# Retention and gated MLP on one core: all weight blocks but three on the transfer queue of the groups, and fewer buffers for keys and decays

## The chip, the cores and the metric

One NeuronCore of one Trainium2 chip. The metric is the device time of one execution in microseconds (us), the median of several runs. "Span" is the time from the first to the last instruction of a profiled execution.

## What is computed

A retention layer (linear attention with a decay per head), then a gated MLP whose spatial weight mixes the positions of a sequence. Cut to what matters:

```python
# q, k, v: (4, 8, 768, 64)
for t in range(S):
    state = gamma * state + k[t] (outer) v[t]
    y[t] = scale * q[t] @ state
x = y as (4, 768, 512)
h = maximum(x @ w_in, 0)            # w_in (512, 1024)
u, v = h[..., :512], h[..., 512:]
v_n = (v - mean(v)) / sqrt(var(v) + 1e-6)
v_s = einsum('ts,bsd->btd', w_spatial, v_n) + b_spatial
out = (u * v_s) @ w_out             # w_out (512, 512)
```

## The kernel before, in words

The sequence of each of the 4 batches is cut into 6 chunks of 128 positions: 24 **groups**, G0 to G23. `load_group` (L197) loads one group with four transfers, all issued on SP: `qv` in two halves of 256 KB, `kk` (512 KB: the keys in two layouts) and `qd` (256 KB: decays). GpSimd (POOL) then scales the values in place, one instruction for each half (L214). `ret_set(g)` (S, L216) multiplies the scores of group g+1 and the state update of group g on TensorE (PE); VectorE (DVE) adds the state (L250) and masks the scores (L257). `ret_out(g)` (X, L259) multiplies the outputs; DVE scales them with `qd` (`xf`, L283), ScalarE (ACT) rounds them to `xh` (L286), POOL takes the residue `xl`. So qv of group g is free after X(g) on PE, kk after S(g) on PE, qd after `xf` of g on DVE.

The weights come as doubles. `load_double` (L, L134) loads one of 12 raw blocks of 512 KB (4 of w_inv, 4 of w_inu, 4 of w_out); `split_double` (C, L147) makes two 32-bit halves out of it: abs on ACT (`da`, L154), five instructions on DVE (L155 to L159), a cast on ACT (L160), a residue on DVE for the first four blocks and on POOL for the others, and the low half on POOL (L162). Blocks 0 to 5 have places of their own; the later ones share two staging buffers. `load_spatial` (K) loads the spatial weight (2.25 MB in six transfers `wst`), `split_spatial` (W) splits it with a cast on ACT (L187) and a residue on DVE (on POOL for the last one of 12).

The MLP: `mlp_v` (V, 12 matmuls of 512 columns) and `mlp_norm` (N) make the normalised v: relu on ACT (`vr`, L320), statistics on DVE (`bst`, `mv`), three tiny instructions on POOL (`rs`, `nb`), then the norm, `vnh` (L333) and `vnl` on ACT and DVE. `item` (I) does one unit: `mlp_u` (`u`, relu `ur` on ACT), `mlp_spatial` (`sp`, needs vnh and vnl of all six chunks and all of the spatial weight), `mlp_out` (`o`, needs a block of w_out). Three float32r matmuls stand for each product (high by high, high by low, low by high).

The words of `START`, `FIRST`, `REST` and `LAST` give the program order. A scheduler then orders each engine's instructions, but every load keeps its place among the loads of its queue (`keep_in_program_order`, L115 and L132), and so do the matmuls after START. A queue issues in order: a transfer whose buffer is not free holds back all that stand behind it on that queue. Groups go over SP's queue, weights over ACT's queue, in which the ACT instructions stand too. Stores of the output (L405) are issued on SP as well, and the scheduler places them.

Of the loads of a group, `QD_BUFS` and the `bufs` of `qv` and `kk` say how far ahead they may run; all three are 3 before.

Of the kernel before, what the change touches and what calls it, by code (L numbers as in the profile page):

```python
# [9 lines left out]
F32 = mybir.dt.float32  # L10
# [3 lines left out]
I64 = mybir.dt.int64  # L14
# [12 lines left out]


START = (
    "v m L0 G0 L1 L2 L3 G1 C0 C1 S-1 G2 L4 L5 C2 S0 X0 C3 S1 X1 G3 V0 C4 S2 X2 V1 C5 G4 K0 S3 X3 "  # L30
    "N0 V2 K2 N1 V3 G5 S4 X4 N2 K4 K5 V4 N3 B U5 X5 N4 V5 L6 L7 W00 W10 W20 N5 W30 W40 W50"
)
FIRST = (
    "C6 I0 G6 C7 L8 W01 C8 L9 I1 G7 W11 W21 Z5 C9 L10 I2 S6 W31 G8 C10 L11 I3 X6 S7 W41 W51 G9 C11 "
    "I4 X7 S8 G10 I5 X8 S9 G11 I6 X9 S10 G12 V0 V1 I7 X10 S11 N0 V2 N1 V3 N2 G13 X11 V4 N3 V5 N4 O7 "
    "N5"
)
# [4 lines left out]
LAST = "I0 I1 I2 I3 I4 I5 I6 I7 O7"  # L42


BLOCKS = [0, 1, 2, 3, 4, 5, 6, 8, 7, 9, 10, 11]
VECTOR_BLOCKS = 4
VECTOR_SPATIAL = 11
WARM_UP = 10
QD_BUFS = 3


@with_exitstack
def tile_retention_gmlp(
# [14 lines left out]
    nc = tc.nc  # L68
    P = 128
    B = out.shape[0]  # L70
    NG = kk.shape[0]
    NC = NG // B
    C = P // 2
    D = C
    NP = kk.shape[2] // (4 * D)
    S = NC * P
    KT = w_inv.shape[1]
    DM = KT * P
    NJ = KT
    HALF = S // 2  # L80
# [5 lines left out]
    rpool = ctx.enter_context(tc.tile_pool(name="ret", bufs=2))  # L86
    mpool = ctx.enter_context(tc.tile_pool(name="mlp", bufs=2))
# [6 lines left out]
    bsp_t = wpool.tile([P, S], F32, name="bsp_t")  # L94
# [7 lines left out]
    wsp_h = wpool.tile([P, NC, S], F32R, name="wsp_h")  # L102
    wsp_l = wpool.tile([P, NC, S], F32R, name="wsp_l")
# [10 lines left out]
    def load(dst, src):  # L114
        tc.keep_in_program_order(nc.sync.dma_start(dst, src))  # L115

    def residue(eng, out, whole, high):
        eng.tensor_tensor(out, whole, high.bitcast(F32), ALU.subtract)  # L118

    def pick(on_vector):  # L120
        return nc.vector if on_vector else nc.gpsimd

    doubles = [
        (w[:, k, 0], w[:, k, 1], src[:, k])
        for w, src in ((winv_w, w_inv), (winu_w, w_inu), (wout_w, w_out))
        for k in range(KT)
    ]
# [3 lines left out]
    def load_weight(dst, src):  # L131
        tc.keep_in_program_order(nc.scalar.dma_start(dst, src))  # L132

    def load_double(i):  # L134

        if i >= len(doubles):
            return
        if i < 6:
            tag = ("vnh", "vnl")[i // 3]
            if i % 3 == 0:  # L140
                raws[tag] = mpool.tile([P, 3, DM], I64, tag=tag, name=f"raw{i}", bufs=1)
            raws[i] = raws[tag][:, i % 3]
        else:
            raws[i] = mpool.tile([P, DM], I64, tag="raw", name=f"raw{i}")[:, :]
        load_weight(raws[i], doubles[i][2])

    def split_double(i):  # L147
        hi, lo, _ = doubles[i]
# [17 lines left out]
    def load_spatial(c):  # L166


        if c < 4:
            if c % 2 == 0:  # L170
                tag = ("xh", "xl")[c // 2]
                t = mpool.tile([P, 2, S], F32, tag=tag, name=f"wst{c}", bufs=3)
                load_weight(t, w_sp[:, c : c + 2])
                for i in range(2):
                    for half in range(2):
                        staged[c + i, half] = t[:, i, half * HALF : half * HALF + HALF]
        elif c < NC:
            for half in range(2):
                tag = ("t", "gh" if half else "gl")[c - 4]
                t = mpool.tile([P, HALF], F32, tag=tag, name=f"wst{c}_{half}")  # L180
                load_weight(t, w_sp[:, c, half * HALF : half * HALF + HALF])
                staged[c, half] = t[:, :]

    def split_spatial(c, half):
        cols = slice(half * HALF, half * HALF + HALF)
        whole = staged.pop((c, half))
        nc.scalar.copy(wsp_h[:, c, cols], whole)  # L187
        residue(pick(c + NC * half < VECTOR_SPATIAL), wsp_l[:, c, cols], whole, wsp_h[:, c, cols])

    queries = {}  # L190
    keys = {}
# [5 lines left out]
    def load_group(g):  # L197
        if g >= NG:
            return

        t = rpool.tile([P, 4, 2, NP, C], F32, tag="qv", name=f"qv{g}", bufs=3)
        kt = rpool.tile([P, 2, 2, NP, C], F32, tag="kk", name=f"kk{g}", bufs=3)
        qd = rpool.tile([P, NP, P], F32, tag="qd", name=f"qd{g}", bufs=QD_BUFS)
        for r in range(2):
            rows = t[ROWS[r], 2 * r : 2 * r + 2]
            load(rows.rearrange("p s i h c -> p (s i h c)"), qv[g, r])
        load(kt[:, :, :, :, :].rearrange("p s i h c -> p (s i h c)"), kk[g])
        load(qd, qdecay[g % NC])
        queries[g], keys[g], naturals[g] = (t[:, 2], t[:, 1]), kt[:, 0], kt[:, 1]
        values[g], decays[g] = (t[:, 0], t[:, 3]), qd  # L210
        for r in range(2):
            vd = vd_t[ROWS[r], g % NC].unsqueeze(3).broadcast_to([D, 2, NP, D])
            w = values[g][r][ROWS[r]]
            nc.gpsimd.tensor_tensor(w, w, vd, ALU.mult)  # L214
# [195 lines left out]
    def item(b, i):  # L410
# [21 lines left out]
        "O": lambda b, g, n: mlp_out(b, *units[n]),  # L432
        "m": lambda b, g, n: load(mask_t, mask),
        "v": lambda b, g, n: load(vd_t, vdecay),
        "B": lambda b, g, n: load_weight(bsp_t, b_sp),
    }

    def emit(text, b, g0):
# [85 lines left out]
```

## Time and profile before

| | |
|---|---|
| median of 3 runs | 439.87 us (438.54 to 441.08) |
| the profiled execution's own time | 439.42 us |
| its span | 437.6 us |
| PE busy | 383.7 us (88%) |
| DVE / POOL / ACT busy | 218.2 / 174.7 / 128.7 us |
| mean granted PE clock | 0.938 of full |
| moved by DMA | 47.44 MB |

In the page's 40 slices (10.9 us each) PE is at 8 tenths or less in most of the first twelve and at 9 or more nearly throughout after them, but for one slice around 240 us. DVE is at 9 from the third to the sixth slice. The rows further down are in us from the start of the span; "idle before" is the time that an engine stood before an instruction, and what ended it.

### The profile page before, as it was taken

Reading aid. Unit: us, or ns where it says so; the run is one execution under the profiler, and the core shown is the slowest. Engines: PE = TensorE matmul, PEld = TensorE weight load, DVE = VectorE, ACT = ScalarE, POOL = GpSimd, SP = SyncE. Lnnn points to the kernel's source line nnn. Section 1 sums busy time; section 2 is a strip of 40 time slices with the busy share of each in tenths; the row PEclk is TensorE's granted clock in tenths of the full one; section 3 lists DMA queues with packets and bytes.
Section 4 is the critical chain, followed back from the end, with each engine's and each line's share of the span. In section 5 each row is a group of like instructions: output and inputs, shape, how many; then the busy total and the mean of one; then the engine's idle time right before and its main releaser. Section 6 shows DMA issues by size and latency. Waiting matters only on the chain.

```text
span 437.6 us, 9093 instructions
## 1 busy us (share of the span) xinstructions
PE 383.7 (88%) x3786; PEld 338.0 (77%) x3786; DVE 218.2 (50%) x420; ACT 128.7 (29%) x231; POOL 174.7 (40%) x201
## 2 busy tenths in 40 slices
PE   3278964888897999999995799999999999999996
PEld 1156652787786988799994788898999988999995
DVE  4699995468775555455552223354554124322122
ACT  3122534433222114542112013451113124511212
POOL 1666765564544444634442222424352223211110
PEclk8588686889998999999999799999999999999999
DMA  8974659511244542164434500064441000100102
GB/s 245 284 246 122 195 191 272 173 48 54 94 121 124 158 154 61 63 193 121 146 99 148 166 0 1 0 191 124 124 121 73 0 1 0 73 0 1 73 0 73
DMA packets 17417, 47.44 MB, mean 108 GB/s; under 512 B 2528, under 2 KB 3296, under 8 KB 17376
## 3 DMA queue, kind: packets, MB, share of 16 engines
q1 hardware_dynamic: 14640, 37.81, 28.6%
q10 hardware_dynamic: 2736, 9.05, 6.7%
q8 instruction: 30, 0.49, 0.5%
q14 instruction: 11, 0.09, 0.1%
HBM read 40.56 MB, written 6.29 MB: 107 GB/s over the span
## 4 chain that ended last, share of the span: by engine, by line
PE 75%; DMA 9%; DVE 7%; POOL 3%; issue 2%; ACT 2%; SPq 1%; POOLq 0%; DVEq 0%; ACTq 0%
PE sp L110 21%; PE v L110 15%; PE o L110 14%; PE u L110 14%; PE s L110 6%; PE x L110 5%; DMA qv<-in_qv_dram 3%; DMA qd<-in_qdecay_dram 2%; DMA raw<-in_w_inu_dram 2%; DVE qv L257 1%; DMA kk<-in_kk_dram 1%; DVE df L157 1%; DMA raw<-in_w_out_dram 1%; POOL xl L118 1%; DVE qv L250 1%
## 5 line engine op out<-in xcount | busy, mean ns | idle before, releaser
L214 POOL TENSOR_TENSOR qv<-qv,vd_t 64x512 f32<-64x512 f32 x48 | 54.3, 1132 | 57.1 <-DMA qv<-in_qv_dram 49.8
L118 POOL TENSOR_TENSOR gl<-t,gh 128x384 fp32r<-128x384 f32 x31 | 31.5, 1016 | 111.5 <-ACT gh L380 110.4
L110 PE MATMUL u<-xh,winu_w 128*128 128x384 f32 x256 | 72.6, 347 | 1.9 <-POOL winu_w L162 1.9
L110 PE MATMUL sp<-wsp_h,vnh 128*128 128x384 f32 x192 | 64.9, 338 | 3.2 <-ACT ur L354 3.2
L110 PE MATMUL v<-winv_w,xh 128*128 128x512 f32 x192 | 65.4, 423 | 0.9 <-POOL winv_w L162 0.7
L110 PE MATMUL o<-wout_w,gh 128*128 128x512 f32 x192 | 61.1, 398 | 5.0 <-POOL wout_w L162 5.0
L110 PE MATMUL sp<-wsp_h,vnl 128*128 128x384 f32 x192 | 64.9, 338 | 0.0
L110 PE MATMUL sp<-wsp_l,vnh 128*128 128x384 f32 x192 | 64.9, 338 | 0.0
L378 DVE TENSOR_TENSOR t<-sp,bsp_t 128x384 f32<-128x384 f32 (+1 forms) x34 | 18.0, 534 | 90.9 <-PE sp L110 90.8
L110 PEld LDWEIGHTS u<-xh,winu_w 128*128 128x128 f32 x256 | 47.3, 190 | 3.9 <-POOL winu_w L162 2.3
L110 PE MATMUL s<-qv,kk 64*64 64x64 f32 x1440 | 31.5, 233 | 17.6 <-DMA kk<-in_kk_dram 13.2
L110 PEld LDWEIGHTS v<-winv_w,xh 128*128 128x128 f32 x192 | 38.8, 206 | 9.8 <-POOL winv_w L162 0.8
L110 PE MATMUL v<-winv_w,xl 128*128 128x512 f32 x96 | 40.7, 424 | 5.7 <-POOL xl L118 5.7
L110 PEld LDWEIGHTS o<-wout_w,gh 128*128 128x128 f32 x192 | 36.0, 189 | 11.6 <-POOL wout_w L162 5.8
L110 PEld LDWEIGHTS s<-qv,kk 64*64 64x64 f32 x1440 | 27.7, 144 | 21.5 <-issue 19.4
L380 ACT CAST gh<-t 128x384 fp32r<-128x384 f32 (+1 forms) x34 | 16.6, 493 | 92.5 <-DVE t L379 90.1
L257 DVE TENSOR_TENSOR qv<-s,mask_t 64x256 f32<-64x256 f32 x92 | 38.6, 420 | 10.1 <-PE s L110 8.7
L110 PE MATMUL u<-xl,winu_w 128*128 128x384 f32 x128 | 43.3, 338 | 0.0
L118 POOL TENSOR_TENSOR xl<-xf,xh 128x512 fp32r<-128x512 f32 x24 | 31.3, 1303 | 29.7 <-ACT xh L286 29.7
L110 PEld LDWEIGHTS x<-qv 128*64 128x64 f32 (+1 forms) x768 | 27.9, 146 | 16.5 <-DVE qv L250 8.3
L110 PEld LDWEIGHTS sp<-wsp_h,vnh 128*128 128x128 f32 x192 | 36.6, 191 | 3.6 <-ACT ur L354 3.5
L110 PE MATMUL x<-qv 128*64 128x64 f32 (+1 forms) x768 | 32.9, 236 | 6.4 <-DVE qv L250 6.1
(57 smaller groups left out, 525.9 us busy)
## 6 DMA issues: line engine op xcount, KB each, us to landing
qv<-in_qv_dram SPq DMA_DIRECT2D x48, 256.0 KB, 4.3
kk<-in_kk_dram SPq DMA_DIRECT2D x24, 512.0 KB, 5.6
qd<-in_qdecay_dram SPq DMA_DIRECT2D x24, 256.0 KB, 5.5
out_dram<-ot SPq DMA_DIRECT2D x23, 256.0 KB, 2.0
raw<-in_w_inv_dram ACTq DMA_DIRECT2D x4, 512.0 KB, 6.9
raw<-in_w_inu_dram ACTq DMA_DIRECT2D x4, 512.0 KB, 7.0
raw<-in_w_out_dram ACTq DMA_DIRECT2D x4, 512.0 KB, 3.8
wst<-in_w_sp_dram ACTq DMA_DIRECT2D x2, 768.0 KB, 6.2
```

Of the source, the lines that this page charges most:

```text
L110: ins = nc.tensor.matmul(out, lhs, rhs, start=start, stop=stop)
L118: eng.tensor_tensor(out, whole, high.bitcast(F32), ALU.subtract)
L157: nc.vector.scalar_tensor_tensor(fi, top, -0x40000000, ai, ALU.bitwise_and, ALU.bitwise_or)
L214: nc.gpsimd.tensor_tensor(w, w, vd, ALU.mult)
L250: nc.vector.tensor_tensor(dst, u, w[r][ROWS[1 - r], i], ALU.add)
L257: nc.vector.tensor_tensor(m[r][ROWS[r], i], ts[i][col, 0], mk, ALU.mult)
L378: nc.vector.tensor_tensor(t[:, c], pp[:, c], bsp_t[:, tc_], ALU.add)
L380: nc.scalar.copy(gh[:, c], t[:, c])
```

## The change

- Raw blocks 0 to 8, the spatial weight and `b_sp` are loaded on SP's queue, among the groups; raw blocks 9 to 11 stay on ACT's queue (`FIRST_QUEUE`).
- Raw blocks from 6 on have three staging buffers where they had two.
- `kk` and `qd` have two buffers where they had three.
- START and FIRST are written anew: groups 1 to 5 come later between the weights, group 6, the spatial weight, and raw blocks 6 to 8 are loaded within START, and 9 to 11 early in FIRST. REST and LAST stay.
- The last residue of the spatial weight goes from POOL to DVE.

```diff
 START = (
-    "v m L0 G0 L1 L2 L3 G1 C0 C1 S-1 G2 L4 L5 C2 S0 X0 C3 S1 X1 G3 V0 C4 S2 X2 V1 C5 G4 K0 S3 X3 "
-    "N0 V2 K2 N1 V3 G5 S4 X4 N2 K4 K5 V4 N3 B U5 X5 N4 V5 L6 L7 W00 W10 W20 N5 W30 W40 W50"
+    "v m L0 G0 C0 L1 L2 S-1 C1 G1 L3 C2 S0 X0 G2 C3 L4 L5 S1 X1 K0 V0 C4 G3 S2 X2 K2 V1 C5 N0 G4 L6 "
+    "S3 X3 V2 N1 G5 W00 W10 K4 K5 S4 X4 V3 N2 W20 W30 B V4 N3 L7 U5 X5 W40 W50 N4 V5 G6 N5 L8"
 )
 FIRST = (
-    "C6 I0 G6 C7 L8 W01 C8 L9 I1 G7 W11 W21 Z5 C9 L10 I2 S6 W31 G8 C10 L11 I3 X6 S7 W41 W51 G9 C11 "
+    "C6 L9 I0 C7 W01 L10 C8 I1 G7 W11 W21 Z5 L11 C9 I2 S6 W31 G8 C10 I3 X6 S7 W41 W51 G9 C11 "
...
+FIRST_QUEUE = 9
 VECTOR_BLOCKS = 4
-VECTOR_SPATIAL = 11
+RAW_BUFS = 3
+KK_BUFS = 2
 WARM_UP = 10
-QD_BUFS = 3
+QD_BUFS = 2
...
-            raws[i] = mpool.tile([P, DM], I64, tag="raw", name=f"raw{i}")[:, :]
-        load_weight(raws[i], doubles[i][2])
+            raws[i] = mpool.tile([P, DM], I64, tag="raw", name=f"raw{i}", bufs=RAW_BUFS)[:, :]
+        (load if i < FIRST_QUEUE else load_weight)(raws[i], doubles[i][2])
...
-                load_weight(t, w_sp[:, c : c + 2])
+                load(t, w_sp[:, c : c + 2])
...
-                load_weight(t, w_sp[:, c, half * HALF : half * HALF + HALF])
+                load(t, w_sp[:, c, half * HALF : half * HALF + HALF])
...
-        residue(pick(c + NC * half < VECTOR_SPATIAL), wsp_l[:, c, cols], whole, wsp_h[:, c, cols])
+        residue(nc.vector, wsp_l[:, c, cols], whole, wsp_h[:, c, cols])
...
-        kt = rpool.tile([P, 2, 2, NP, C], F32, tag="kk", name=f"kk{g}", bufs=3)
+        kt = rpool.tile([P, 2, 2, NP, C], F32, tag="kk", name=f"kk{g}", bufs=KK_BUFS)
...
-        "B": lambda b, g, n: load_weight(bsp_t, b_sp),
+        "B": lambda b, g, n: load(bsp_t, b_sp),
```

PE's order stays nearly the same. Three places show what moves elsewhere. Numbers behind names are the group or block (`qv3` is of G3) and a buffer's serial number; lines of the changed kernel are three higher than before.

**SP's queue from group 2 on.** Before, groups alone:

```order
L115 DMA qv2_166<-in_qv_dram 64x1024 x2
L115 DMA kk2_167<-in_kk_dram 128x1024
L115 DMA qd2_168<-in_qdecay_dram 128x512
L115 DMA qv3_327<-in_qv_dram 64x1024 x2
L115 DMA kk3_328<-in_kk_dram 128x1024
```

In the changed kernel:

```order
L118 DMA qv2_242<-in_qv_dram 64x1024 x2
L118 DMA kk2_243<-in_kk_dram 128x1024
L118 DMA qd2_244<-in_qdecay_dram 128x512
L118 DMA raw3_164<-in_w_inu_dram 128x512 x2
L118 DMA wst0_327<-in_w_sp_dram 128x1536
L118 DMA qv3_366<-in_qv_dram 64x1024 x2
L118 DMA kk3_367<-in_kk_dram 128x1024
L118 DMA qd3_368<-in_qdecay_dram 128x512
L118 DMA wst2_438<-in_w_sp_dram 128x1536
```

Two raw blocks (4 and 5, in one tile named raw3) and a third of the spatial weight now stand between groups 2 and 3, and qd2 ahead of them waits for `xf` of group 0.

**DVE around the output of group 1.** Before:

```order
L250 TENSOR_TENSOR qv2_166<-s1_1_265,qv1_113 64x256 x2
L257 TENSOR_TENSOR qv2_166<-s1_1_265,mask_t_73 64x256 x2
L283 TENSOR_TENSOR xf1_323<-x1_306,qd1_115 128x512
L155 TENSOR_SCALAR da4_362<-da4_362 128x512
L321 BN_STATS bst0_0_352<-vr0_0_351 128x6
```

In the changed kernel:

```order
L253 TENSOR_TENSOR qv2_242<-s1_1_265,qv1_155 64x256 x2
L260 TENSOR_TENSOR qv2_242<-s1_1_265,mask_t_73 64x256 x2
L121 TENSOR_TENSOR wsp_l_81<-wst0_327,wsp_h_80 128x384 x4
L286 TENSOR_TENSOR xf1_323<-x1_306,qd1_157 128x512
L158 TENSOR_SCALAR da4_355<-da4_355 128x512
```

Four residues of the spatial weight, which need the transfer wst0, now stand ahead of `xf` of group 1; four more follow around group 2 and four around group 4.

**ACT from the relu of the last two v chunks to the first units.** Before:

```order
L320 ACTIVATE vr0_5_763<-v0_5_750 128x512
L132 DMA raw6_774<-in_w_inu_dram 128x512
L332 ACTIVATE vr0_4_699<-vr0_4_699,nb0_4_708,rs0_4_702 128x512
L132 DMA raw7_776<-in_w_out_dram 128x512
L333 CAST vnh0_336<-vr0_4_699 128x512
L154 ACTIVATE da6_793<-raw6_774 128x512
L332 ACTIVATE vr0_5_763<-vr0_5_763,nb0_5_772,rs0_5_766 128x512
L333 CAST vnh0_336<-vr0_5_763 128x512
L154 ACTIVATE da7_869<-raw7_776 128x512
L354 ACTIVATE ur0_0_0_817<-u0_0_0_804 128x384
```

In the changed kernel:

```order
L135 DMA raw9_815<-in_w_out_dram 128x512
L323 ACTIVATE vr0_5_779<-v0_5_766 128x512
L157 ACTIVATE da8_888<-raw8_802 128x512
L357 ACTIVATE ur0_0_0_830<-u0_0_0_817 128x384
L335 ACTIVATE vr0_4_710<-vr0_4_710,nb0_4_719,rs0_4_713 128x512
L357 ACTIVATE ur0_1_0_845<-u0_1_0_832 128x384
L335 ACTIVATE vr0_5_779<-vr0_5_779,nb0_5_788,rs0_5_782 128x512
L336 CAST vnh0_329<-vr0_4_710 128x512
L163 CAST wout_w_82<-df7_874 128x512
L336 CAST vnh0_329<-vr0_5_779 128x512
```

Raw blocks 6 and 7 were issued here and used at once; now they, and block 8, are loaded before, and only blocks 9 to 11 are issued from here on.

## Rows read from the trace of the kernel before

**Rows 1.** Busy time by stretch: PE, PEld, DVE, ACT, POOL, PE clock, DMA, GB/s
```profile
5.75:10.00 4.25, 0.00 (x0) 0.00 (x0) 3.63 (x8) 1.72 (x3) 0.00 (x0) 0.79 1.05 294
10.00:20.00 10.00, 1.61 (x36) 1.26 (x36) 6.42 (x9) 1.06 (x3) 8.36 (x6) 0.50 1.03 287
20.00:26.72 6.72, 3.98 (x95) 3.73 (x97) 6.41 (x15) 1.79 (x4) 3.37 (x3) 0.60 0.94 286
26.72:35.49 8.77, 6.29 (x112) 4.58 (x111) 8.42 (x15) 2.34 (x4) 5.30 (x4) 1.00 0.49 145
35.49:70.28 34.79, 26.22 (x370) 19.74 (x370) 33.18 (x60) 13.38 (x25) 21.65 (x23) 0.80 0.65 193
```

**Rows 2.** What PE waited for from 60 to 140 us: total, times, longest
```profile
PE v L110 <- POOL xl L118: 5.1, 1, 5.1
PE o L110 <- POOL wout_w L162: 5.0, 2, 3.4
PE sp L110 <- ACT ur L354: 3.2, 1, 3.2
PE u L110 <- POOL winu_w L162: 1.9, 1, 1.9
```

**Rows 3.** Chain of waits over the first 160 us: start, duration, what
```profile
73.76 8.18 PE v L110 x22
...
81.97 4.26 DMA raw<-in_w_inu_dram
...
93.83 4.25 DMA raw<-in_w_inu_dram
...
100.52 3.81 DMA raw<-in_w_out_dram
```

**Rows 4.** Chain of waits from 215 to 246 us
```profile
216.44 1.09 PE s L110 x64
...
237.17 5.74 DMA kk<-in_kk_dram
```

**Rows 5.** Timeline of ACT: the first raw blocks, and chunk 5's norm
```profile
0.72 1.86 ACTq L132 DMA_DIRECT2D raw<-in_w_inv_dram  x4
...
86.82 0.80 ACT L332 ACTIVATE vr<-vr,nb,rs 128x512 f32<-128x512 f32 x1
87.66 0.62 ACT L333 CAST vnh<-vr 128x512 fp32r<-128x512 f32 x1
...
88.74 0.86 ACT L354 ACTIVATE ur<-u 128x384 f32<-128x384 f32 x2
```

**Rows 6.** Timelines of SP (first group, a steady turn) and DVE (that turn)
```profile
1.64 1.17 SPq L115 DMA_DIRECT2D qv<-in_qv_dram  x2
...
208.03 0.58 SPq L115 DMA_DIRECT2D kk<-in_kk_dram  x1
...
206.89 0.69 DVE L283 TENSOR_TENSOR xf<-x,qd 128x512 f32<-128x512 f32 x1 [2.00 <-PE x L110]
```

**Rows 7.** Issues of `kk` in 0 to 15 and 140 to 230 us: median us to landing
```profile
kk<-in_kk_dram SPq DMA_DIRECT2D x2, 512.0 KB, 8.6
...
kk<-in_kk_dram SPq DMA_DIRECT2D x8, 512.0 KB, 5.0
```

**Rows 8.** DVE's groups to 90 us, by shape: busy, mean ns, idle before
```profile
L118 DVE TENSOR_TENSOR wsp_l<-wst,wsp_h 128x384 fp32r<-128x384 f32 x11 | 7.0, 654 | 5.3 <-ACT wsp_h L187 5.2
```

**Rows 9.** Timeline of POOL: `xl` of chunk 4, and the scaling of group 9
```profile
72.45 1.26 POOL L118 TENSOR_TENSOR xl<-xf,xh 128x512 fp32r<-128x512 f32 x1
...
128.52 2.49 POOL L214 TENSOR_TENSOR qv<-qv,vd_t 64x512 f32<-64x512 f32 x2 [2.11 <-DMA qv<-in_qv_dram]
```

**Rows 10.** Timeline of PE: ends of the first `sp` and of the second `o`
```profile
94.10 0.34 PE L110 MATMUL u<-xh,winu_w 128*128 128x384 f32 x1
...
113.75 1.16 PE L110 MATMUL s<-qv,kk 64*64 64x64 f32 x64
```

**Rows 11.** Chain near the end: two `u` units
```profile
375.60 4.19 PE u L110 x24
```

## The prediction

> **What bounds the kernel now.** I first read the busy time by stretch, to split the program into stages, then what PE waited for, then the chain of waits, and last the timelines of POOL, ACT and SP at the places that the change touches. After some 140 us PE is the bound and the change adds nothing to its work, so all that can be won lies before. There are two stages in it.
>
> In the first, up to the end of `xf` of the sixth chunk at 70.28 us, VectorE is the bound. From its first weight instruction at 5.75 it is busy 3.63 + 6.42 + 6.41 + 8.42 + 33.18 = 58.06 of 64.53 us; from 20 us on it idles 2.3 us in all [rows 1]. DMA is not: it moved 286 GB/s until 26.7 us and then only 145 and 193 [rows 1].
>
> In the second, from 70 to 134 us, PE waits for things that come late: 5.1 us for `xl` behind POOL, 3.2 for a relu that ACT reaches late, 1.9 for a block of w_inu and 5.0 for two of w_out [rows 2]. The chain says why: the three raw blocks on it are each issued only when they are due, and their transfers take 4.26, 4.25 and 3.81 us with the split behind them [rows 3]. A further stop stands at 237 us, where group 18 waits behind stores on SP's queue [rows 4]; REST and the order of those stores are unchanged, so I leave it as it is.
>
> **The change part by part.**
>
> *Start of the program.* The first raw block was issued on ACT at 0.72 [rows 5]. It now comes third on SP, where the third issue stood at 1.64 [rows 6]: 0.9 us later. DVE so starts near 6.7. In exchange one raw block instead of four stands ahead of the first group. DVE's idle time before 20 us, 0.6 + 3.6 in [rows 1], mostly goes: up to the first `xf` it has 16.5 us of the same work, so I place that at 23.5 with 0.3 us for waits, where it was 26.7.
>
> *The first stage after it.* qd2 waits for this `xf`, since `qd` has two buffers, and behind it stand 1.0 MB of raw blocks and 0.75 MB of the spatial weight. A group's 1.0 MB takes 1.16 us of issue and 5.0 to land [rows 6, 7]; less 3.5 us for its bytes at 286 GB/s [rows 1] this leaves 2.7 us for start and landing. So the first third of the spatial weight is there at 23.5 + 2.7 + 2.0 MB at 286 GB/s (7.0) = 33.2, and its first cast by 33.7. DVE takes its next 8.8 us of work [rows 1], reaches the four residues moved ahead of the second `xf` at 32.3, and waits 1.4 us. They cost 4 x 0.654 = 2.6 [rows 8], so the second `xf` starts at 36.3 against 35.49. From there the same 34.8 us follow, again with eight residues in them: 71.1, where it was 70.28. **The 3 us won at the start are spent on four residues and a wait: the first stage gives about nothing.** Bounds: DVE without any gap would end at 6.7 + 58.06 + 2.6 = 67.4, 3 us better; the other end is a rival below. I stay near 71, because the wait is worked out from a measured rate. What is won is work done ahead: all spatial residues but none late, and raw blocks 6 to 8 loaded.
>
> *Chunk 4's `xl`.* Before it ended at 72.45 + 1.26 = 73.71 [rows 9], since POOL had to scale groups 6 and 7 first. Now only group 6 stands ahead. Its qv goes out behind qd5, the last third of the spatial weight, the bias and raw block 7: 2.4 MB after the fourth `xf`, which I place at 55.5. That is 55.5 + 2.7 + 8.4 = 66.6, and scaling takes 2.5 [rows 9]: 69.1. The fifth `xf` and its cast come near 68. With up to 1 us of slack `xl` ends at 71.4: **2.3 us earlier.** The 22 matmuls behind it took 8.18 [rows 3], which I keep.
>
> *From the last v to the end of the first `sp`.* This was 94.10 - 81.94 = 12.2 us [rows 3, 10]; ACT stood before the abs of raw block 6 until its transfer, issued there, had landed. Now nothing in ACT's order waits for a transfer there. Two u units take 4.2 at full clock [rows 11]; behind the second one ACT does a relu (0.43), a norm (0.80), two casts of v and one of a weight (3 x 0.62) [rows 5], DVE a residue (0.7), PE the last matmul: 8.4 us. **3.8 us earlier.** At least 4.2 + 3.1 are needed by PE alone, at most it stays as it was.
>
> *To the end of the second `o`.* 113.75 - 94.10 = 19.65 us [rows 10] with the waits for blocks of w_inu (1.9) and w_out (5.0 - 3.4 = 1.6) in them [rows 2]. Block 8 is there early; 9 to 11 are issued on ACT some 20 us ahead of their matmuls, into three buffers. Both waits go: **3.5 us earlier.** If the splits rather than the transfers set them, nothing goes.
>
> *The last wait, 3.4 us.* The low half of the last w_out block stands on POOL behind the scaling of group 9 (2.49 us, after 2.11 us idle for its transfer) [rows 9]. Now that qv goes out behind qd8, which waits for an `xf` (0.7) and moves 0.9 us of bytes; the block's residue, 1.3 us, moves ahead of the scaling. I take nothing for it; it can at most give back the 3.4.
>
> *Fewer buffers later.* In a steady turn kk was issued at 208.03. Now qd of the group before goes first, after an `xf` that ends at 207.58 [rows 6]; with 0.4 and 1.2 us of issue kk goes at 209.2 and lands by 214.2 to 215.1, with qd's bytes ahead. Its scores are due at 216.44 [rows 4]. Hidden, by 1.3 to 2.2 us; if this cover were gone, PE would wait in every turn. The buffer of kk itself is free 1.1 us after X, earlier than this. The residue of the spatial weight moved to DVE costs 0.65 in the first stage, within the 2.6 above.
>
> The sum: -2.3 - 3.8 - 3.5 = -9.6, against the profiled execution's 439.42 (span 437.6 plus 1.8 around it): **429.8 us**. That execution lies 0.45 under the median of 439.87, so the changed kernel's median may as well be 430.
>
> **The rivals.**
>
> *More goes.* DVE closes all gaps of the first stage (3.0) and the wait for the last w_out block goes too (3.4): 423.4. For it: POOL does that block's residue earlier. Against: qd2's place on the queue.
>
> *One queue delays the groups.* With ACT's and SP's queues both loaded, a kk took 8.6 us to land against 5.0 in a quiet stretch [rows 7], so bytes are shared in the start either way. In one queue group 3 stands behind all 1.75 MB of weights. Were it served in turn with them it would be through after 2.5 MB instead of 3.0: 1.75 us at 286 GB/s. If groups 3, 4 and 5 each come that much after DVE wants them, 5.2 us go: 435.0. Against: I have kk3 and kk4 there about when DVE comes to them. The Trainium skill states such a service in turn ("DMA: Bandwidth & Descriptors", section "Queues, rings and completion order"): each DMA engine alternates packet by packet between the queue rows that have work, so that two queues share and one queue does not. By that rule the old queues favoured the groups and this change takes that away; no run here shows one row alone in the start.
>
> *Slower: the short buffers.* If kk needs over 216.44 - 209.2 = 7.2 us to land in the steady turns, PE stops in each. With the crowded 8.6 [rows 7] that is 1.4 us in each of 11 such groups, 15.4 in all: 439.42 - 9.6 + 15.4 = 445. Against: 5.0 was measured there with the same bytes.
>
> *The early loads do not help.* The blocks are there, but ACT, in order, has block 8's abs ahead of the first relu, and that waits for a buffer which POOL frees behind the scaling of groups 7 and 8. If those land 6 us later than I think, the second stage's 7.3 us shrink to 1, and the first gives nothing: about 438.5.
>
> **How the numbers follow.** My forecast has 0.50 (425.5 to 433), more goes 0.15, one queue delays 0.17, early loads do not help 0.10, slower 0.08. A difference within 0.5%, 2.2 us, can hardly be told from no change. Faster by more: 0.50 + 0.15 + 0.17 = 0.82. Within: 0.09. Slower: 0.09, with the tail of the fourth case. The range takes in the forecast, most of "more goes" and the delayed queue: 422.5 to 437.
>
> **What would show it.** In the changed profile DVE should be busy from 7 to 70 us nearly without a gap but for 1 to 2 us before a residue of the spatial weight near 33. No raw block should stand on the chain after 75 us. PE's waits for `ur`, for winu_w and the shorter one for wout_w should be gone, and the second `o` should end near 104. The stop of group 18 should stand unchanged, some 10 us earlier. I am wrong if kk or qv appears among PE's waits in the steady turns, if `xf` of the sixth chunk ends after 74 or before 67, or if waits for winu_w and wout_w remain with no transfer behind them.

## The result and the profile after

The changed kernel takes **442.10 us** (median of 20 runs, 439.64 to 446.42) against 439.96 for the kernel before in the same session: a ratio of 1.0049, with an interval from 1.0026 to 1.0072. That is 0.5% slower, where 429.8 was forecast and 437 was the end of the range. The profiled execution took 439.64 us with a span of 437.8, 2.5 us under that median, so its stages show where time moved rather than the exact sum.

| | before | forecast | after |
|---|---|---|---|
| end of the first `xf` | 26.72 | 23.5 | 26.89 |
| end of the second `xf` | 36.18 | 37.0 | 42.64 |
| end of the sixth `xf` | 70.28 | 71.1 | 80.17 |
| from there to the end of the second `o` | 43.47 | 33.05 | 37.27 |
| end of the second `o` | 113.75 | 104.15 | 117.44 |

Between the sixth `xf` and the second `o` it gained 6.2 us where 10.4 were forecast; up to the sixth `xf` it lost 9.9, and an end of that `xf` after 74 was one of the prediction's own signs of being wrong. Of the 3.7 us that are late at the second `o`, this execution makes up 3.5 by its end (0.8 at the last w_out block, 1.0 at the stop of group 18, the rest spread over the turns); by the medians it is less. The windows of the first stage show how. Columns are PE, PEld, DVE, ACT, POOL, PE clock, DMA share, GB/s, as in [rows 1]. Before:

```profile
22.00:28.00 6.00, 4.37 (x141) 4.03 (x136) 5.68 (x13) 2.02 (x4) 3.85 (x4) 0.72 0.89 287
28.00:38.00 10.00, 7.41 (x118) 5.67 (x118) 9.72 (x16) 2.50 (x4) 5.91 (x5) 0.88 0.54 143
38.00:44.00 6.00, 4.69 (x44) 3.56 (x42) 5.82 (x12) 1.22 (x2) 4.60 (x6) 0.92 0.43 141
```

In the changed kernel:

```profile
22.00:28.00 6.00, 2.17 (x64) 2.04 (x64) 5.78 (x12) 1.28 (x2) 3.58 (x4) 0.50 0.06 22
28.00:38.00 10.00, 5.90 (x52) 4.17 (x46) 6.51 (x12) 0.79 (x2) 2.23 (x2) 0.84 1.01 299
38.00:44.00 6.00, 3.30 (x81) 3.14 (x82) 5.62 (x8) 3.25 (x7) 3.10 (x3) 0.54 0.10 29
```

Twice for 6 us the DMA engines move 22 and 29 GB/s, and in between 299, with VectorE (DVE) idle for a third of those 10 us, where it was busy 9.72 of them before. (Idle DMA engines need not cost anything: before, they moved 4 GB/s from 33 to 36 us, with DVE busy 2.85 of those 3 us.) SP's timeline in the changed kernel tells why:

```profile
19.64 0.33 SPq L118 DMA_DIRECT2D kk<-in_kk_dram  x1
26.91 0.33 SPq L118 DMA_DIRECT2D qd<-in_qdecay_dram  x1
27.30 0.90 SPq L118 DMA_DIRECT2D raw<-in_w_inu_dram  x2
28.24 0.43 SPq L118 DMA_DIRECT2D wst<-in_w_sp_dram  x1
28.84 1.19 SPq L118 DMA_DIRECT2D qv<-in_qv_dram  x2
30.13 0.69 SPq L118 DMA_DIRECT2D kk<-in_kk_dram  x1
42.66 0.33 SPq L118 DMA_DIRECT2D qd<-in_qdecay_dram  x1
```

kk2 goes out at 19.64, then nothing for 7 us: qd2 is next, and its buffer is that of qd0, which the first `xf` reads until 26.89. Behind it stand the raw blocks, the spatial weight and group 3. The same recurs with qd3 at 42.66, behind the second `xf`. DVE's timeline shows the price; the last bracket is idle time and what ended it:

```profile
38.38 3.66 DVE L121 TENSOR_TENSOR wsp_l<-wst,wsp_h 128x384 fp32r<-128x384 f32 x4 [3.65 <-ACT wsp_h L190]
41.96 0.68 DVE L286 TENSOR_TENSOR xf<-x,qd 128x512 f32<-128x512 f32 x1
```

The third of the spatial weight issued at 28.24 landed at 37.8; DVE stood 3.65 us before its first residue, with the second `xf` behind it, and four residues took 3.66 us where [rows 8] gave 2.6. How long PE waited for `kk` ahead of scores (`s`) up to 60 us, before and in the changed kernel (total, times, longest):

```profile
PE s L110 <- DMA kk<-in_kk_dram: 5.7, 2, 4.1
PE s L113 <- DMA kk<-in_kk_dram: 16.2, 3, 6.5
```

What it waited for from 60 to 140 us, where [rows 2] stood, in the changed kernel:

```profile
PE v L113 <- ACT xh L289: 4.3, 1, 4.3
PE sp L113 <- ACT vnh L336: 2.7, 1, 2.7
PE o L113 <- POOL wout_w L165: 2.6, 1, 2.6
PE s L113 <- DMA kk<-in_kk_dram: 2.0, 1, 2.0
PE sp L113 <- ACT ur L357: 1.6, 1, 1.6
```

The wait for winu_w is gone and that for wout_w fell from 5.0 to 2.6 us, where 3.4 was forecast; that for `ur` fell only from 3.2 to 1.6, and the wait for `vnh` is new. POOL's timeline shows what was late there:

```profile
87.76 1.18 POOL L217 TENSOR_TENSOR qv<-qv,vd_t 64x512 f32<-64x512 f32 x1 [0.46 <-DMA qv<-in_qv_dram]
88.91 1.26 POOL L165 TENSOR_TENSOR winu_w<-df,da 128x512 fp32r<-128x512 f32 x1
90.26 0.23 POOL L326 TENSOR_SCALAR rs<-mv 128x1 f32<-128x1 f32 x1
90.57 1.04 POOL L217 TENSOR_TENSOR qv<-qv,vd_t 64x512 f32<-64x512 f32 x1
...
94.67 0.27 POOL L329 TENSOR_SCALAR nb<-mv,rs 128x1 f32<-128x1 f32 x1
```

The last v's relu ended at 87.2, and its `nb` only at 94.9: on POOL the tiny statistics stand behind the scaling of group 8, whose transfer was issued at 80.64 behind a held qd7 (80.20), and behind a weight's sum.

### The profile page after: what moved, and what is told of

Same layout as the page of the kernel before. It is cut to its first block, busy times and chain, and to the rows that moved or that the text cites. A ratio compares the mean times of both kernels' runs of the same rounds, so it can differ in the third digit from the quotient of the medians.

```text
span 437.8 us, 9095 instructions
## 1 busy us (share of the span) xinstructions
PE 383.7 (88%) x3786; PEld 338.7 (77%) x3786; DVE 229.8 (52%) x421; ACT 128.9 (29%) x231; POOL 173.5 (40%) x200
## 4 chain that ended last, share of the span: by engine, by line
PE 66%; DVE 12%; DMA 9%; POOL 4%; issue 4%; ACT 3%; SPq 1%; POOLq 0%; DVEq 0%; ACTq 0%
PE sp L113 21%; PE u L113 15%; PE o L113 14%; PE v L113 8%; PE s L113 4%; PE x L113 4%; DMA qv<-in_qv_dram 4%; DMA wst<-in_w_sp_dram 3%; DVE qv L260 2%; DVE wsp_l L121 2%; POOL qv L217 1%; DVE xf L286 1%; DVE df L160 1%; DMA raw<-in_w_inv_dram 1%; SPq L118 1%
## 5 line engine op out<-in xcount | busy, mean ns | idle before, releaser
L217 POOL TENSOR_TENSOR qv<-qv,vd_t 64x512 f32<-64x512 f32 x48 | 53.3, 1111 | 67.6 <-DMA qv<-in_qv_dram 63.9
L121 POOL TENSOR_TENSOR gl<-t,gh 128x384 fp32r<-128x384 f32 x31 | 31.9, 1028 | 106.3 <-ACT gh L383 104.7
L113 PE MATMUL u<-xh,winu_w 128*128 128x384 f32 x256 | 73.9, 352 | 0.0
L113 PE MATMUL v<-winv_w,xh 128*128 128x512 f32 x192 | 64.0, 415 | 5.0 <-ACT xh L289 4.7
L113 PE MATMUL s<-qv,kk 64*64 64x64 f32 x1440 | 33.4, 245 | 28.9 <-DMA kk<-in_kk_dram 24.6
L113 PEld LDWEIGHTS s<-qv,kk 64*64 64x64 f32 x1440 | 29.7, 155 | 32.5 <-issue 31.5
L113 PEld LDWEIGHTS u<-xh,winu_w 128*128 128x128 f32 x256 | 48.5, 195 | 1.7
L113 PEld LDWEIGHTS v<-winv_w,xh 128*128 128x128 f32 x192 | 37.4, 200 | 13.7 <-ACT xh L289 5.2
L260 DVE TENSOR_TENSOR qv<-s,mask_t 64x256 f32<-64x256 f32 x92 | 38.6, 420 | 8.8 <-PE s L113 7.7
L113 PEld LDWEIGHTS o<-wout_w,gh 128*128 128x128 f32 x192 | 35.7, 188 | 8.7 <-POOL wout_w L165 3.0
L113 PE MATMUL v<-winv_w,xl 128*128 128x512 f32 x96 | 39.1, 408 | 0.9 <-POOL xl L121 0.9
L113 PE MATMUL o<-wout_w,gl 128*128 128x512 f32 x96 | 37.7, 393 | 0.0
L113 PEld LDWEIGHTS sp<-wsp_h,vnl 128*128 128x128 f32 x192 | 36.4, 190 | 1.5 <-DVE vnl L121 1.5
```

The costliest lines, as they stand in the source:

```text
L113: ins = nc.tensor.matmul(out, lhs, rhs, start=start, stop=stop)
L260: nc.vector.tensor_tensor(m[r][ROWS[r], i], ts[i][col, 0], mk, ALU.mult)
```

## The experiments

Four theories stood. **Q**: a decay held at the head of the one queue holds everything behind it. **O**: the four residues ahead of the second `xf` cost by their place. **C**: DVE's instructions take longer while POOL works. **P**: in the second stage POOL's order is the bound. The runs in one table (times in us; ratio to the kernel before on the same chip, with its interval). They come from four sessions, in which the median of the kernel before lay between 439.14 and 440.58, so two runs are best compared by their ratios. And the scheduler orders DVE, ACT and POOL anew for every edit; only e11 left the order of everything that it did not move as it was.

| kernel | 2nd `xf` | 6th `xf` | median | ratio |
|---|---|---|---|---|
| before | 36.2 | 70.3 | 439.96 | |
| changed | 42.6 | 80.2 | 442.10 | 1.0049 (1.0026 to 1.0072) |
| e1_qd3 | 37.6 | 75.3 | 434.58 | 0.9893 (0.9851 to 0.9936) |
| e3_actq | 39.6 | 78.9 | 439.30 | 0.9986 (0.9954 to 1.0017) |
| e4_klate | 35.6 | 77.5 | 440.54 | 1.0026 (0.9998 to 1.0054) |
| e5_klate_qd3 | 35.8 | 71.5 | 433.21 | 0.9849 (0.9813 to 0.9884) |
| e6_before_early67 | 36.7 | 71.4 | 437.35 | 0.9943 (0.9914 to 0.9973) |
| e7_before_qd2 | 35.2 | 75.9 | 443.57 | 1.0086 (1.0055 to 1.0117) |
| e8_noscale | 35.2 | 73.4 | 432.88 | 0.9841 (0.9802 to 0.9880) |
| e9_lateres | 36.1 | 72.3 | 438.02 | 0.9911 (0.9877 to 0.9945) |
| e10_late_on_dve | 37.1 | 72.6 | 428.32 | 0.9725 (0.9688 to 0.9763) |
| e11_last_on_dve | 36.3 | 71.4 | 432.06 | 0.9812 (0.9773 to 0.9852) |
| e12_actq_qd3 | 41.8 | 81.1 | 438.99 | 0.9957 (0.9930 to 0.9984) |
| e13_c11 | 35.6 | 71.4 | 423.54 | 0.9641 (0.9623 to 0.9660) |

### One more decay buffer (e1_qd3)

```diff
-QD_BUFS = 2
+QD_BUFS = 3
```

> The changed kernel with a third buffer for the decays (qd), nothing else different. Theory Q (held queue): qd of group g+2 waits on the one queue for the xf of chunk g, and what stands behind it starts late. Then the two stretches without transfers at 22 to 28 and 39 to 44 us go, the first third of the spatial weight lands near 31 us instead of 37.9, VectorE no longer idles 3.65 us before the first residue, the second xf ends near 38.5 (was 42.6), the sixth near 75 (was 80.2), and the time falls by 4 to 5 us to about 437.5. Rival C (VectorE is full and its instructions are longer because POOL works beside it): the idle time goes, but the instructions stay long or grow; the sixth xf ends at 78 or later, the time falls by less than 2 us. Rival O (the order: four residues ahead of the second xf): of 3.65 us of waiting some goes, the residues stay; the same as C for the time, with VectorE's own durations unchanged.

Its windows over the first two of these stretches:

```profile
22.00:28.00 6.00, 1.88 (x56) 1.75 (x60) 5.76 (x11) 1.28 (x2) 3.55 (x4) 0.50 0.97 353
28.00:38.00 10.00, 7.68 (x138) 5.81 (x132) 9.69 (x18) 2.96 (x6) 4.55 (x4) 0.92 1.01 284
```

22 GB/s became 353, DVE's 6.51 of 10 us became 9.69, the sixth `xf` ended at 75.3, as Q said, and the time fell by 7.5 us (6.9 by the ratios), some 3 more than Q said: the second stage got shorter too (33.4 us from the sixth `xf` to the second `o`, 3.9 less than in the changed kernel); group 8 was issued at 74.62, 0.7 us ahead of the sixth `xf` and not 0.5 behind it. **One constant turns the changed kernel from 0.5% slower to 1.1% faster.** Q is shown, with one limit: from the first to the second `xf` e1 takes 10.5 us and the changed kernel 15.8, but from the second to the sixth both take the same, 37.7 and 37.5. So the first hold has the whole price of the first stage, and those of qd3 to qd5 have none there, though the second one empties the DMA engines just as long. kk2, which also waited for its buffer (issued at 19.64, 7.0 us behind the qv ahead of it), was not given back its third one by any run.

### Two decay buffers in the kernel before (e7_before_qd2)

```diff
-QD_BUFS = 3
+QD_BUFS = 2
```

> The kernel before with one part of the change alone: two buffers for the decays instead of three. Theory Q says that a decay that waits for an xf holds what stands behind it on SP's queue. Here only groups stand there, the weights being on ACT's queue: group 3 is issued after the first xf (26.7 us) instead of earlier, and lands near 33 to 34, which the second xf at 36.2 leaves little room for. Q: the second xf ends 1 to 3 us later, the time rises by 1 to 4 us, to 441 to 444. If the two buffers cost only together with the weights in the same queue: within 1 us of 440. If two buffers by themselves are what the change loses: 445 or more.

The time rose by 0.86%, some 3.8 us, in the range of Q, but not where I put it: the second `xf` was not late, so that agreement is luck. qd5 went out at 55.31, after the fourth `xf`, and the values of group 6 behind it at 55.76; they landed 9.79 us later. POOL's scaling of them held up a norm, ACT stood 5.74 us before that norm, and the last third of the spatial weight, issued by ACT behind it, began to go out at 68.22 (before: 65.22). Its first piece landed at 74.18, and here the scheduler had put one residue of it ahead of the sixth `xf`, where it stood behind that `xf` before: DVE idled 3.49 us for it, and the `xf` ended 5.6 us late. So the hold is there without the one queue, carried on by two engines that work in order, but most of the 5.6 us in this run is that one residue's place.

### The weights on ACT's queue again (e3_actq, e12_actq_qd3)

```diff
-FIRST_QUEUE = 9
+FIRST_QUEUE = 0
...
-                load(t, w_sp[:, c : c + 2])
+                load_weight(t, w_sp[:, c : c + 2])
...
```

> The changed kernel with all raw blocks, the spatial weight and the bias issued on ACT's queue again; order and buffers are the changed ones. Theory Q: a held qd on SP no longer holds the weights; the first third of the spatial weight lands before 32 us and the stretches without transfers get shorter, but the groups still wait for their own qd, and ACT, in order, pays the issues: 437 to 441, about 2 us better than the changed kernel. If the one queue is what costs all (groups and weights in one row served in order), the sixth xf ends near 71 as before, and the time is near 433. Rival C: no transfer matters, the sixth xf ends near 79, the time stays within 1.5 us of 442.

> The changed kernel with three decay buffers, and the raw blocks, the spatial weight and the bias on ACT's queue again. Theory Q says that one queue costs only while something is held at its head: with three buffers two queues give no more than one, 433 to 436, about the 434.6 of the kernel with the one queue. The rival of the prediction (one queue delays the groups, because weights stand ahead of them): the second and third xf end 1.5 us or more earlier than with the one queue (37.7 and 49.8), and the time is under 432. Slower than 437: ACT pays for the issues.

The edit of e12 differs from that of e3 by the third decay buffer, and from that of e1 by the queue alone. With two buffers the second queue gains 2.8 us (0.6%), as Q expected; with three it loses 2.8 by the ratios (0.6%; 4.4 between the medians), where Q had expected no difference: the outcome is the last one named, slower than 437. So the single queue is not what costs: the second `xf` came at 41.8, not earlier than 37.6. The stretch from 10 to 20 us, in e1:

```profile
10.00:20.00 10.00, 3.25 (x102) 3.12 (x103) 9.81 (x17) 3.27 (x6) 4.61 (x4) 0.50 1.04 323
```

and in e12:

```profile
10.00:20.00 10.00, 4.08 (x112) 3.76 (x112) 3.98 (x9) 0.66 (x1) 3.30 (x3) 0.50 1.02 271
```

DVE has work for 9.81 of 10 us in the first and for 3.98 in the second, with the DMA engines full in both (1.04 and 1.02). DVE lives on raw blocks here, and where these are issued tells most of the difference. SP in e1:

```profile
4.41 1.26 SPq L118 DMA_DIRECT2D raw<-in_w_inv_dram  x2
20.89 1.92 SPq L118 DMA_DIRECT2D raw<-in_w_inu_dram  x2
```

ACT in e12:

```profile
7.86 0.62 ACT L163 CAST winv_w<-df 128x512 fp32r<-128x512 f32 x1 [1.68 <-DVE df L160]
7.86 2.76 ACTq L135 DMA_DIRECT2D raw<-in_w_inv_dram  x2
37.67 0.82 ACTq L135 DMA_DIRECT2D raw<-in_w_inu_dram  x2
```

ACT comes to the second and third raw block only behind its own work on the first, 3.5 and 5.3 us later than SP, and to blocks 4 and 5 some 17 us later: ACT pays for the issues. Sharing is the smaller part. The Trainium skill ("DMA: Bandwidth & Descriptors", section "Queues, rings and completion order") has each DMA engine go round the queues for which it has work. The landings agree: in e12 those two raw blocks took 10.1 and 11.0 us from issue to landing (8.0 and 9.3 in e1), and `kk` of groups 1 to 3 landed 1.0 to 1.6 us earlier than in e1. I took that rule for a danger to this change. One queue does delay the groups by that much, but DVE does not stand for it: in e1 it idles 4.1 us in all from its first weight instruction to the sixth `xf`, against 6.5 before. Whether a second queue would help if its loads were listed ahead of ACT's work, no run shows.

### Spatial weight later in the start (e4_klate, e5_klate_qd3)

The middle of START; e5 has `QD_BUFS = 3` besides:

```diff
-S1 X1 K0 V0 C4 G3 S2 X2 K2 V1 C5 N0 G4 L6 S3 X3 V2 N1 G5 W00 W10 K4 K5 S4 X4 V3 N2 W20 W30 B
+S1 X1 V0 C4 G3 S2 X2 V1 C5 N0 G4 K0 L6 S3 X3 V2 N1 G5 K2 W00 W10 S4 X4 V3 N2 W20 W30 K4 K5 B
```

> The changed kernel with the loads of the spatial weight later in the start (after groups 4 and 5 and after the first of their splits are listed), so that less stands ahead of groups 3 to 5; qd keeps two buffers. Rival O (four residues ahead of the second xf, and the weight ahead of group 3): the second xf ends near 36.5 instead of 42.6, the sixth near 75, time about 437. Theory Q: qd2 still waits for the first xf, group 3 still stands behind qd2 and two raw blocks: group 3 lands near 36, the second xf ends near 38 (nothing but its own scores ahead of it), but the residues come later and the waits behind qd3 to qd5 stay: the sixth xf near 78, time 440 or more.

> Both edits together: three buffers for the decays, and the loads of the spatial weight later in the start. Theory O (the four residues ahead of the second xf cost by their place): the second xf ends near 35.5 instead of 37.7, and some of it reaches the sixth xf: near 73.5, time near 432.5. If VectorE is simply full up to the sixth xf, the residues cost the same wherever they stand ahead of it: the second xf ends earlier, the sixth stays within 1 us of 75.3, and the time within 1.5 us of 434.6.

With the decay still held (e4) the second `xf` came 7 us earlier and at most 1.6 us were left of it at the end, as Q said: O holds at its place only. The price of the hold moved with the weight: from the second to the sixth `xf` e4 takes 41.8 us and e5, with the third buffer, 35.7. With three buffers (e5) the sixth `xf` came 3.8 us earlier than in e1, so the place does count (the residues took 0.71 us each instead of 0.91). But the second `o` ended at 108.8 (e1: 108.7), and the times, 434.58 and 433.21, can't be told apart. After the sixth `xf` something else decides; see P.

### Without POOL's early scaling (e8_noscale)

```diff
-            nc.gpsimd.tensor_tensor(w, w, vd, ALU.mult)
+            if g >= 8:
+                nc.gpsimd.tensor_tensor(w, w, vd, ALU.mult)
```

> The changed kernel with three buffers for the decays, and without POOL's scaling of the values by the decay for the first eight groups: that part of the computation is left out. Theory C (VectorE's instructions with two operands in SBUF, or of the single-operand kind, take two to four times as long while POOL works): VectorE's busy time up to the sixth xf falls from 63.6 us to 58 or less, the mean of the 12 residues of the spatial weight from 0.91 to under 0.7, and the sixth xf ends at 71 or earlier instead of 75.3. Without C: the busy time stays within 1.5 us of 63.6, and the sixth xf moves only by what waits for POOL, under 2 us.

This run, like e1 with three decay buffers, leaves out part of the computation: the values of the first eight groups stay unscaled. DVE's groups from 7.4 to 72 us (busy, mean ns), in e1:

```profile
L121 DVE TENSOR_TENSOR wsp_l<-wst,wsp_h 128x384 fp32r<-128x384 f32 x12 | 10.5, 911 | 0.8 <-ACT wsp_h L190 0.8
L253 DVE TENSOR_TENSOR qv<-s,qv 64x256 f32<-64x256 f32 x18 | 7.6, 423 | 0.6
L161 DVE TENSOR_SCALAR da<-df 128x512 int32<-128x512 int32 x6 | 4.1, 682 | 0.1
```

and here:

```profile
L254 DVE TENSOR_TENSOR qv<-s,qv 64x256 f32<-64x256 f32 x20 | 8.4, 422 | 0.6
L121 DVE TENSOR_TENSOR wsp_l<-wst,wsp_h 128x384 fp32r<-128x384 f32 x12 | 7.8, 682 | 5.3 <-ACT wsp_h L190 5.3
L161 DVE TENSOR_SCALAR da<-df 128x512 int32<-128x512 int32 x6 | 2.5, 424 | 0.1
```

With POOL busy 22.1 instead of 38.6 us, the same 108 instructions of DVE up to the sixth `xf` take 56.1 us instead of 63.6. Most of those that read only SBUF, with one or two operands, get shorter on average; those that read PSUM (`s`) stay at 0.42 us. C is shown, and its price is 7.5 us of DVE's time. The sixth `xf` ended only 1.9 us earlier, though: DVE then waited 5.3 us for the spatial weight. The transfers stand right behind DVE.

The means hide what happens. Three residues of e1 on DVE, and POOL beside them:

```profile
38.76 0.56 DVE L121 TENSOR_TENSOR wsp_l<-wst,wsp_h 128x384 fp32r<-128x384 f32 x1 [0.78 <-ACT wsp_h L190]
39.57 2.72 DVE L121 TENSOR_TENSOR wsp_l<-wst,wsp_h 128x384 fp32r<-128x384 f32 x2
39.31 2.56 POOL L217 TENSOR_TENSOR qv<-qv,vd_t 64x512 f32<-64x512 f32 x2 [4.27 <-DVE wsp_l L121]
```

The first, begun with POOL idle, took 0.56 us; the other two, each begun while a scaling was running, took 1.40 each. So it is with all twelve: seven took 0.52 to 0.56 us, and the five that began while a scaling or a residue was running on POOL took 1.39 to 1.51. Over all fourteen traces, up to 76 us, the SBUF instructions of the weights' splits and of `vnl` on DVE number 697: of the 212 that began while a scaling, a residue or a sum was running on POOL 203 took over 0.15 us longer than alone, of the other 485 two. The time lost so up to the sixth `xf` adds up to 10.0 us before, 13.5 in e1 and 6.0 in e8; the last two differ by the 7.5 us. The Trainium skill ("SBUF — State Buffer", section "SBUF: two separate sides") states the cause: the two engines share a pair of ports to SBUF, and for DVE instructions in a two-port mode or with two inputs in SBUF the engine that starts first has it for its whole instruction, while the other waits. The durations above agree.

### Residues held back (e9_lateres)

On top of e1, the residues (now ordered by a pin among the `xf`) come where the program lists them:

```diff
-        residue(nc.vector, wsp_l[:, c, cols], whole, wsp_h[:, c, cols])
+        tc.keep_in_program_order(
+            nc.vector.tensor_tensor(
+                wsp_l[:, c, cols], whole, wsp_h[:, c, cols].bitcast(F32), ALU.subtract
+            )
+        )
...
-        nc.vector.tensor_tensor(
-            xf, t[:, :, :, :].rearrange("p n i c -> p n (i c)"), decays.pop(g), ALU.mult
+        tc.keep_in_program_order(
+            nc.vector.tensor_tensor(
+                xf, t[:, :, :, :].rearrange("p n i c -> p n (i c)"), decays.pop(g), ALU.mult
+            )
         )
```

> The changed kernel with three buffers for the decays, and the residues of the spatial weight held in the order in which the program lists them among the xf, so that 5 instead of 12 stand ahead of the sixth xf. If VectorE is the bound up to the sixth xf (13 us of POOL's and PE's work lie beside it, none of it longer), 7 residues at the 0.91 us that they took are 6.4 us less work there: the sixth xf ends near 70, and the time is 429 to 431, if the 7 residues then lie beside PE's work. Rival: the wait for values that POOL scales or for the next group takes the place: the sixth xf ends at 73 or later and the time stays within 1.5 us of 434.6. Slower is possible where a residue now holds up VectorE between the last v and the first sp: over 437.

The sixth `xf` moved by 3.1 of the 6.4 us, and PE then waited 4.1 us for `wsp_l` in `sp`: the second `o` ended at 109.5, 0.8 later than in e1. The forecast of 429 to 431 failed; by the ratios the time is 0.2% over that of e1, which can't be told from none. Work that is taken off DVE ahead of the sixth `xf` is lost again if it lands between there and the first `sp`.

### One part alone in the kernel before (e6_before_early67)

The end of START:

```diff
-N0 V2 K2 N1 V3 G5 S4 X4 N2 K4 K5 V4 N3 B U5 X5 N4 V5 L6 L7 W00 W10 W20 N5 W30 W40 W50
+N0 V2 K2 L6 N1 V3 G5 S4 X4 N2 L7 K4 K5 V4 N3 B U5 X5 N4 V5 W00 W10 W20 N5 W30 W40 W50
```

> The kernel before with one thing of the change alone: raw blocks 6 and 7 (of w_inu) are loaded early, among the raw blocks of the start, on ACT's queue; order, queues and buffers otherwise as before. What the prediction said of the second stage (a raw block that is issued when it is due costs PE 3.8 us between the last v and the first sp, and the waits for w_inu) holds if the time falls by 3 to 5 us, to 435 to 437, with the first sp ending near 90.5 and the sixth xf still near 70.5. Rival P (the chain there is POOL's and ACT's own order, and the transfer only hid it): the first sp ends within 1 us of 94.1 and the time stays within 1.5 us of 440.

The time fell by 2.5 us (0.57%), but the first `sp` ended at 94.8 instead of 94.3: PE waited 4.7 us for `vnh` there. In the trace the gain comes behind it, where the wait for winu_w is gone (second `o` at 111.5 instead of 113.8). That trace is of the slowest of this kernel's twelve executions (441.31, median 437.35), so it shows the place rather than the size. The transfer was one of two things that were late at that place; that POOL's statistics were the other is argued here, and e10 shows it.

### POOL's order in the second stage (e10_late_on_dve, e11_last_on_dve, e13_c11)

In e5 POOL was busy 12.39 of 13.14 us from 74.00 to 87.14. Part of its timeline:

```profile
81.55 1.04 POOL L217 TENSOR_TENSOR qv<-qv,vd_t 64x512 f32<-64x512 f32 x1
82.67 1.62 POOL L165 TENSOR_TENSOR winu_w<-df,da 128x512 fp32r<-128x512 f32 x1
84.38 0.54 POOL L326 TENSOR_SCALAR rs<-mv 128x1 f32<-128x1 f32 x1
```

The statistics of the last v were ready when its `mv` ended at 79.85; POOL came to them at 84.38. e10 and e11 put the last two steps of raw blocks on DVE, on top of e5 (e11 with `i == 11`):

```diff
-        residue(pick(i < VECTOR_BLOCKS), f, f, hi)
-        nc.gpsimd.tensor_tensor(lo, f, a, ALU.add)
+        residue(pick(i < VECTOR_BLOCKS or i >= 6), f, f, hi)
+        pick(i >= 6).tensor_tensor(lo, f, a, ALU.add)
```

> The kernel with three decay buffers and the later loads of the spatial weight, and the last two steps of raw blocks 6 to 11 (residue and sum) on VectorE instead of POOL. Theory P (between the sixth xf and the second o, POOL's order sets the pace: statistics of the last two v units stand behind scalings and behind these two steps of 1.3 and 1.6 us): the wait for the last w_out block (3.6 us) goes, and the norms of the last v units come about 2 us earlier: 428 to 430. Rival: VectorE has no room there or is itself lengthened, and the norms wait for POOL's scalings all the same: the wait for w_out shrinks to 1 to 2 us and the rest stays: 431 to 434.

> As the run beside it, but only the last raw block (the low half of the last w_out block) has these two steps on VectorE. What the prediction said of the last wait holds if it is the scaling of group 9 ahead of it on POOL that sets it: the wait for wout_w falls from 3.6 to under 1.5 us, the time by 2 to 3 us, to 430 to 431. Rival: VectorE reaches the block's own steps late (they end near 124.8 us), and POOL's scaling was only next to it: the wait stays over 2.5 us and the time within 1 us of 433.2.

e10 gained 4.9 us on e5 and its second `o` ended at 104.7, 4.1 earlier. PE's wait for `vnh` from 60 to 140 us, in e5 and in e10:

```profile
PE sp L113 <- ACT vnh L336: 3.6, 1, 3.6
PE sp L113 <- ACT vnh L336: 0.2, 1, 0.2
```

In e10 POOL began the statistics of the last v at 83.43, 0.21 us after it had run out of work and as soon as their input was there. In e11, where blocks 6 to 10 stay on POOL, the wait for `vnh` is 3.7, and the time can't be told from that of e5. P is shown. But the wait for the last w_out block stayed in e10:

```profile
PE o L113 <- DVE wout_w L165: 3.5, 1, 3.5
```

In e11 it fell only from 3.6 to 2.6 us. So POOL's place for the block's two steps, behind the scaling of group 9, was about 1 us of it. DVE's own order set the rest: the block's steps stood behind an `xf` for which DVE idled 2.1 us. e13 lists them ahead of it, on top of e10 (the end of the first line of FIRST):

```diff
-Z5 L11 C9 I2 S6 W31 G8 C10 I3 X6 S7 W41 W51 G9 C11
+Z5 L11 C9 I2 S6 W31 G8 C10 I3 C11 X6 S7 W41 W51 G9
```

> The fastest kernel so far (three decay buffers, later loads of the spatial weight, blocks 6 to 11 finished on VectorE) with the split of the last raw block listed ahead of the xf of chunk 7 instead of behind the scores that follow it. There PE waited 3.5 us for this block, and VectorE had idled 2.1 us for that xf just ahead of the block's steps. If VectorE's order is what sets the wait, it goes: 424 to 425.5. If the block's transfer, issued late, sets it: the wait moves to VectorE ahead of these steps, holds up the xf and the scores behind them too, and the time is 428 to 431.

PE's waits from 60 to 140 us have no w_out left; the two longest:

```profile
PE v L113 <- ACT xh L289: 5.3, 2, 4.0
PE x L113 <- DVE qv L253: 1.3, 1, 1.3
```

At **423.54 us** this is the fastest kernel of the study, 3.6% under the kernel before.

## Why the prediction was wrong, step by step

**"The first stage gives about nothing" failed; it lost 9.9 us.** The text saw that qd2 waits for the first `xf` and that weights stand behind it, and priced this hold as "waits 1.4 us". DVE stood 3.65 us, and e1 prices the hold at 4.9 us of the sixth `xf` and 7.5 of the time. The sum had the right chain and three terms too small. Against the forecast 71.1 the sixth `xf` was 9.1 us late: 3.4 came with the first `xf`, from which the transfer was counted; 2.3 arose up to the second, where the spatial weight landed 10.9 us after the first `xf` and not 9.7, and its four residues took 3.7 us and not 2.6; and 3.4 in "the same 34.8 us", which took 38.2. Nor does "DMA is not" the bound hold for the start: up to 20 us its share was 1.05 and 1.03 [rows 1], while DVE idled 4.2 us.

The other 5.0 us of the first stage, still there in e1, are terms that were mis-sized. DVE starts 1.93 us later in e1 (7.68 against 5.75; the forecast had 0.9, but the block took 5.3 us to land, 1.0 more than before). Its busy time is 5.52 us more (63.57 against 58.05): four more residues cost 6.1 (10.5 against 4.4), not 2.6, as five of the twelve now began while POOL was running; all else nets to -0.6. Its idle time is 2.41 us less. 1.93 + 5.52 - 2.41 = 5.04.

**First `xf` at 23.5 failed, for the same reason as the residues.** "16.5 us of the same work" took 18.99 us of busy time, because more of these instructions began while POOL was running: 4.9 us were lost so up to the first `xf`, 2.3 before. Without the early scaling the same 30 instructions took 15.1. The other 0.9 us are the later start and DVE's waits.

**The second stage's length came out once the first no longer spoils it, but in part by luck.** In e1 it takes 75.3 to 108.7, 33.4 us, against 33.05 forecast and 43.47 before. Two of its three terms missed, by 2.5 us each and in opposite directions: the last v ended 6.0 us after the sixth `xf` (8.5 forecast), the first `sp` 10.9 us after that v (8.4 forecast), and the second `o` 16.5 after that (16.1 forecast). So of the 3.8 us that were to go "from the last v to the end of the first `sp`" 1.3 went in e1, and in the changed kernel, with 14.0 us, none. The sum of 8.4 lists steps of ACT, DVE and PE and puts POOL's three statistics instructions at nothing; these decide there, as e10 shows. In the changed kernel 4.2 us of the forecast were lost in this stage, 3.9 of which come back in e1: groups 7 and 8, themselves behind held decays, reached POOL in the middle of the statistics. What the forecast called the cause, the late raw blocks, was one part of it: e6 alone brings 2.5 us, and e10 shows POOL as the other part, with 4.9.

**"The last wait unchanged"** held in e1 (3.7 us), but for another reason than the text gives: by e11 and e13, which stand on later kernels, the scaling of group 9 is about 1 us of such a wait, and the order of DVE the rest.

**The short buffers in the steady turns** are hidden, as forecast: after 140 us PE waits for kk once, 6.4 us, at the stop that the kernel before had too. The slower rival had its price on the right parts, the shorter buffers, and the wrong place: not the steady turns but the start, and not kk but qd.

**"One queue delays the groups"** did not come about: against e12 the keys of groups 1 to 3 do land 1.0 to 1.6 us later in e1, but DVE never stood long enough for them to lose 5.2 us (it idled 4.1 in all). **"Early loads do not help"** is not borne out by e1 and e6, though its mechanism, ACT behind POOL's scaling of groups 7 and 8, is what the late `vnh` in the changed kernel shows.

## What to carry to other kernels

A transfer that waits for a buffer stops every transfer behind it in its queue, so before loads are put into one queue, list for each one which instruction frees its buffer, and look at what stands behind the ones that wait: one more small buffer (here 2 KB in each partition) was worth 7.5 us. The engine that issues counts too: SP does nothing but issue here, while ACT reaches an issue only behind its own work. And when an engine's time is summed from durations, don't take means: a DVE instruction on SBUF has one duration alone and another when POOL is already running, and what must be forecast is how many meet.

## What was unexpected of the hardware

With POOL's scaling beside them DVE's residues took 34% longer on average (0.91 against 0.68 us) and a single-operand instruction on SBUF 61% (0.68 against 0.42); those on PSUM took no longer (e8). No single one was 34% longer: in e1 a residue took 0.55 us or 1.4, and it took 1.4 when a POOL instruction of 512 columns had begun before it. Beside one of POOL's tiny statistics, of one column, it took 0.52.

In e1 PE stood for 3.7 us before the last w_out block. Its granted clock was 1.00 before, 0.54 (about the lower of its two levels, 1.2 of 2.4 GHz) for the rest of that `o`, and 1.00 after it:

```profile
115.20:117.30 2.10, 2.10 (x12) 1.44 (x12) 1.12 (x2) 0.82 (x2) 0.23 (x1) 1.00 0.00 0
...
128.91:132.30 3.39, 3.39 (x8) 2.48 (x8) 0.00 (x0) 1.58 (x3) 1.01 (x1) 0.54 0.19 74
132.40:140.00 7.60, 7.60 (x128) 7.46 (x128) 3.99 (x9) 1.70 (x3) 2.91 (x3) 1.00 0.78 242
```

Eight matmuls took 3.39 us there; at full clock nine of the same kind began at 115.05 and were followed by the next kind at 117.21, 0.24 us each. So, by an estimate from these rows, that wait cost some 1.5 us more than its own length. In e10 the same fall follows the wait of 3.5 us:

```profile
124.30:127.50 3.20, 2.76 (x7) 2.18 (x8) 1.41 (x3) 1.22 (x3) 0.36 (x1) 0.50 0.01 4
```

In e13, without that wait, the granted clock is 1.00 from 105 to 140 us. That is how removing a wait of 3.5 us could give 3.7 us by the ratios (4.8 between the medians).
